# Turning two row groups of the first batch's spectrum by DMA transposes from a padded tile, and storing the last output rows in two column halves

## Chip, cores, metric

One core of one Trainium2 chip. The metric is the device time of one execution in microseconds (us), lower is better. Times are medians of several executions; all executions quoted here were in the fast state (one core has no die to compare with, and no run lay more than 1.5% above the fastest of its kernel).

## The reference

```python
X = np.fft.rfft(x, axis=1)                        # x: 8 x 3008 x 256, float32
y = np.fft.irfft(X * (filt_r + 1j*filt_i)[None], n=3008, axis=1)
x = y.reshape(24064, 256)
h = x @ w_in                                      # 256 x 2048
g = h * (1.0 / (1.0 + np.exp(-beta * h)))
out = g @ w_out                                   # 2048 x 256
```

## The kernel before

The transform along 3008 is done as a two-stage matrix DFT (64 x 47), in bfloat16. Each batch goes through first-stage products, a transpose, products with the filter between two stages (the "spectrum"), a turn to the other axis, and last products that give `y`. Then comes the two-layer network on `y`. Its unit is a step: two hidden matmuls into `hps`, a Silu on ScalarE, and, two steps later, four output matmuls into `acc`. A step takes TensorE about 0.87 us. (To evacuate is to copy a result out of PSUM, the memory that TensorE writes.) The transform of the next batches is cut into units which `place(first, last, units)` puts between the steps, so that TensorE never stops.

Only the first batch has nothing to hide behind. Its spectrum `z_t` is turned on TensorE, in four groups of 8 rows: group 0 at once, groups 1 to 3 between steps.

```python
    z_t = ypool.tile([P, NDC, J, KP], BF16, name="z_t", tag="y")     # KP = 96 of 128 columns
    ...
    def turn_z(g, i, on_act=False):                                  # half of a group
        if g not in zz0:
            zz0[g] = zzpool.tile([KP, JG, D], BF16, name="zz", tag="zz")
        pz = fpsum.tile([P, 4, D], BF16, name="pz", tag="f")
        for e in range(4):
            for dc in range(NDC):
                nc.tensor.transpose(
                    pz[:KP, e, dc * P : (dc + 1) * P], z_t[:, dc, JG * g + 4 * i + e, :], ident[:]
                )
        evac(zz0[g][:, 4 * i : 4 * i + 4, :], pz[:KP], on_act)       # PSUM to SBUF
    ...
    # one unit of a later batch's spectrum (s23): products, then two units later the inverse stage
            nc.vector.tensor_tensor(p_t[:], ps[:], frr[:, ks_, :], ALU.mult)   # frr: filter
            ...
            nc.gpsimd.tensor_tensor(v_t[:], p_t[:], q_t[:], ALU.add)
            ...
            evac(s["z"][:, kk : kk + 2, :], ps[:], True)             # z: pool of 2 buffers
            if kk + 2 == KG:
                nc.sync.dma_start(s["d2c"][:, g * KG : (g + 1) * KG, :], s["z"][:])
    ...
    place(1, 14, uz(1, True))          # turn + last products of group 1; True: ScalarE evacuates y
    place(15, 29, uz(2, True))
    units = uz(3, True)
    place(20, 24, units[:2], per=2)
    place(34, 58, units[2:])
    ...
        place(10, 10, uf(0, JG), per=9)                              # filter loads, on SyncE
        at = place(9, 14, units[J // 4 :], per=9)                    # second batch, first stage
        place(at + 1, at + 1, [lambda: a2_read(1)] + uf(JG, NK), per=9)   # 8 DMA transposes, loads
        ...
        place(36, 36, ux(2), per=9)                                  # third batch's x, on GpSimd
```

SyncE issues the filter loads, the DMA transposes, the stores of `z` and all output rows, and before the first filter load a small DMA, the "marker", that holds its queue until the second batch's `x` has landed. GpSimd issues the loads of `x`. A queue's "ring" is its row of transfers that are issued and not yet moved. "x load" below is the third batch's, unless said otherwise.

Of the kernel before, what the change touches and what calls it, by code (L numbers as in the profile page):

```python
# [39 lines left out]
def kernel(  # L40
# [396 lines left out]
    z_t = ypool.tile([P, NDC, J, KP], BF16, name="z_t", tag="y")  # L437
# [25 lines left out]
    def inverse3(i):  # L463
        k0 = 2 * i
        p_t, q_t = pq.pop(i)

        last = i == NK // 2 - 1
        for j0, j1 in ((0, JG), (JG, J)) if last else ((0, J),):
            nj = 4 * (j1 - j0)
            if j0:  # L470
                ps = fpsum.tile([P, 2, NDC, nj], F32, name="psz", tag="f")
            else:
                ps = opsum.tile([P, 2, NDC, nj], F32, name="psz", tag="acc")
            for src, tab in ((p_t, t3), (q_t, t3b)):
                for e in range(2):
                    for dc in range(NDC):
                        nc.tensor.matmul(  # L477
                            ps[:, e, dc, :],
                            lhsT=src[:, e, dc * P : (dc + 1) * P],
                            rhs=tab[:, k0 + e, 4 * j0 : 4 * j1],  # L480
                            start=src is p_t and dc == 0 and e == 0,
                            stop=src is q_t,
                            skip_group_check=True,
                        )
            for e in range(2) if last else (None,):
                if last:
                    dst = z_t[:, :, j0:j1, 4 * (k0 + e) : 4 * (k0 + e) + 4]
                    src = ps[:, e].rearrange("p c (j a) -> p c j a", a=4)
                else:
                    dst = z_t[:, :, :, 4 * k0 : 4 * k0 + 8].rearrange(  # L490
                        "p c j (e a) -> p e (c j) a", e=2
                    )
                    src = ps.rearrange("p e c (j a) -> p e (c j) a", a=4)
                evac(dst, src, not last or j0 > 0)
# [45 lines left out]
    zz0[0] = zz0[0][:KP, : JG * D].rearrange("p (j d) -> p j d", j=JG)  # L540


    def turn_z(g, i, on_act=False):
        if g not in zz0:
            zz0[g] = zzpool.tile([KP, JG, D], BF16, name="zz", tag="zz")
        pz = fpsum.tile([P, 4, D], BF16, name="pz", tag="f")
        for e in range(4):
            for dc in range(NDC):
                nc.tensor.transpose(  # L549
                    pz[:KP, e, dc * P : (dc + 1) * P], z_t[:, dc, JG * g + 4 * i + e, :], ident[:]  # L550
                )
        evac(zz0[g][:, 4 * i : 4 * i + 4, :], pz[:KP], on_act)

    def last4(zz, tab, jj, dc, dst, on_act, own=None, first=NP):
        ps = own or fpsum.tile([P, 4, P], F32, name="ps4", tag="f")
        for e in range(4):
            nc.tensor.matmul(  # L557
                ps[:, e, :NP],
                lhsT=zz[:, jj + e, dc * P : (dc + 1) * P],
                rhs=tab[:],  # L560
                start=True,
                stop=True,
            )
        rest = []
        for n0, n1 in ((0, NP),) if own is None or first == NP else ((0, first), (first, NP)):
            rest.append(
                lambda n0=n0, n1=n1: evac(
                    dst[:, n0:n1],
                    ps[:, :, n0:n1].rearrange("p j n -> p n j"),
                    on_act,  # L570
                    inv_scale,
                )
            )
        rest.pop(0)()
        return rest
# [9 lines left out]
    for i in range(4):  # L585
        if i % 2:
            pz = opsum.tile([P, 2, D], BF16, name="pz", tag="acc")
        else:
            pz = fpsum.tile([P, 2, D], BF16, name="pz", tag="f")
        for e in range(2):  # L590
            for dc in range(NDC):
                nc.tensor.transpose(
                    pz[:KP, e, dc * P : (dc + 1) * P], z_t[:, dc, 2 * i + e, :], ident[:]
                )
        evac(zz0[0][:, 2 * i : 2 * i + 2, :], pz[:KP], i % 2 == 1)
# [98 lines left out]
    def zz_read(b):  # L694
        s = st[b]
        s["zz"] = []
        for h in range(NJG):
            t = zzpool.tile([KP, JG, D], BF16, name="zz", tag="zz")
            nc.sync.dma_start(t[:], s["d2r"][:, h * JG : (h + 1) * JG, :])
# [46 lines left out]
    def uz(g, act=False):  # L746
        return [lambda i=i: turn_z(g, i) for i in range(2)] + [
            lambda i=i: last_z(g, i, act) for i in range(2 * NDC)
        ]
# [25 lines left out]
    place(1, 14, uz(1, True))  # L775
    place(15, 29, uz(2, True))
    units = uz(3, True)
    place(20, 24, units[:2], per=2)
    place(34, 58, units[2:])

    first_step = [(S * b // TB) * NFB for b in range(B + 1)]
    if B > 1:
        units = u1(1, True)
        place(3, 8, units[: J // 4], per=2)
        place(10, 10, uf(0, JG), per=9)
        at = place(9, 14, units[J // 4 :], per=9)
        place(at + 1, at + 1, [lambda: a2_read(1)] + uf(JG, NK), per=9)
# [51 lines left out]
    for s in range(len(steps) + LAG):  # L839
# [34 lines left out]
        if s >= LAG:  # L874
# [40 lines left out]
            if fb == NFB - 1:  # L915
                for h, a in enumerate(acc):
# [4 lines left out]
                    if last and h == nch - 1:  # L921
                        for half in range(2):
                            cols = slice(half * P, (half + 1) * P)
                            evac(ost[:, c : c + per, cols], a[:, :, cols], half == 1)
                    else:
                        evac(ost[:, c : c + per, :], a[:], on_act)
# [31 lines left out]
```

## Time and profile before

| | before |
|---|---|
| time, median of the first 3 runs | 776.72 us (776.48 to 778.47) |
| profiled span | 775.3 us |
| TensorE, ScalarE, VectorE busy | 99%, 77%, 49% |
| DMA engines' mean busy share, 64 to 80 us | 70% (below) |

### The profile page before, as it was taken

The page shows a single profiled execution, that of the slowest core. Times are in us where ns is not written, and L with a number is a line of the kernel's source. Part 1 is how long each engine was busy: PE and PEld are TensorE (multiplying, and loading weights), DVE is VectorE, ACT ScalarE, POOL GpSimd, SP SyncE. Part 2 cuts the span into 40 slices and gives each one's busy share as a digit, 9 for nine tenths or more (in the row PEclk, how much of TensorE's full clock was granted, in tenths as well). Part 3 has the DMA queues.
Part 4 walks back from the last instruction along what each step waited for, and adds up shares of the span by engine and source line. Part 5 has one row for each costly group of instructions (what it writes and reads, how often), then busy time and mean ns, then how long its engine had stood idle before and what let it go on. Part 6 is the DMA issues. An engine that isn't in the chain of part 4 may idle for free.

```text
span 775.3 us, 16219 instructions
## 1 busy us (share of the span) xinstructions
PE 767.5 (99%) x6444; PEld 554.2 (71%) x6444; DVE 379.3 (49%) x641; ACT 594.9 (77%) x926; POOL 142.8 (18%) x145
## 2 busy tenths in 40 slices
PE   8999999999999999999999999999999999999998
PEld 4877777777777777877768777787777776776665
DVE  7836846645446553474526735277353761401001
ACT  6888887886678867788677876778767787677776
POOL 7523401420013100231002410034000430000000
PEclk9999999999999999999999999999999999999999
DMA  7969755515911268022761237512451114100101
GB/s 170 240 164 191 169 164 106 136 55 155 177 43 68 89 145 161 30 85 85 160 134 47 78 116 146 106 64 80 130 110 55 49 69 129 56 28 28 55 28 55
DMA packets 103291, 80.48 MB, mean 104 GB/s; under 512 B 48466, under 2 KB 96996, under 8 KB 102258
## 3 DMA queue, kind: packets, MB, share of 16 engines
q1 hardware_dynamic: 100496, 63.73, 30.8%
q0 software_dynamic: 2720, 15.73, 10.5%
q8 instruction: 50, 0.82, 0.5%
q14 instruction: 25, 0.20, 0.1%
HBM read 46.15 MB, written 35.65 MB: 106 GB/s over the span
## 4 chain that ended last, share of the span: by engine, by line
PE 97%; ACT 1%; DMA 1%; POOL 0%; DVE 0%; issue 0%; POOLq 0%
PE acc L907 42%; PE hps L852 42%; PE ps L557 3%; PE ps L628 2%; PE ps L687 2%; PE ps L661 2%; DMA xg<-in_x_dram 1%; PE psz L477 1%; PE pz L549 0%; ACT a L109 0%; ACT a_t L109 0%; PE pb L403 0%; POOL xg L120 0%; PE ps L451 0%; PE ps2q L451 0%; PE pt L354 0%
## 5 line engine op out<-in xcount | busy, mean ns | idle before, releaser
L867 ACT ACTIVATE gT<-hps,beta_sb 128x512 bf16<-128x512 f32 x752 | 516.0, 688 | 166.8 <-PE hps L852 155.0
L907 PE MATMUL acc<-wout_sb,gT 128*128 128x256 bf16 x3008 | 451.6, 272 | 0.0
L852 PE MATMUL hps<-y,win_sb 128*128 128x512 bf16 (+8 forms) x1730 | 447.7, 351 | 0.0
L907 PEld LDWEIGHTS <-gT 128*128 128x128 bf16 x3008 | 279.6, 98 | 106.3 <-ACT gT L867 0.2
L852 PEld LDWEIGHTS <-win_sb 128*128 128x128 bf16 x1730 | 165.0, 98 | 24.4 <-issue 0.2
L677 POOL TENSOR_TENSOR v_t<-p_t,q_t 128x512 bf16<-128x512 f32 x84 | 106.7, 1270 | 383.9 <-DVE q_t L676 375.4
L111 DVE COPY ost<-acc 128x512 f32<-128x512 f32 (+2 forms) x89 | 56.6, 674 | 194.0 <-PE acc L907 188.4
L111 DVE CAST a<-ps 128x384 bf16<-128x384 f32 x96 | 53.5, 558 | 91.4 <-PE ps L628 91.2
L113 DVE TENSOR_SCALAR y<-ps 128x376 bf16<-128x376 f32 (+1 forms) x115 | 61.7, 544 | 59.5 <-PE ps L557 59.5
L672 DVE TENSOR_TENSOR p_t<-ps,frr 128x512 f32<-128x512 f32 x84 | 58.1, 692 | 33.5 <-PE ps L661 30.9
L676 DVE TENSOR_TENSOR q_t<-ps,fri 64x512 f32<-64x512 f32 x84 | 58.3, 694 | 1.2
L673 DVE SCALAR_TENSOR_TENSOR q_t<-ps,fri 64x512 f32<-64x512 f32 x84 | 57.4, 684 | 1.1
L557 PEld LDWEIGHTS <-zz 96*128 96x128 bf16 x512 | 35.3, 97 | 29.1 <-issue 0.3
L109 ACT ACTIVATE z<-ps 128x512 bf16<-128x512 f32 x84 | 49.6, 590 | 0.0
L628 PEld LDWEIGHTS <-xg 94*128 94x128 bf16 x448 | 30.7, 97 | 23.4 <-issue 0.4
L628 PE MATMUL ps<-t1b,xg 94*128 94x96 bf16 x448 | 36.7, 205 | 0.0
L557 PE MATMUL ps<-t,zz 96*128 96x94 bf16 x448 | 36.7, 204 | 0.0
L687 PE MATMUL ps<-v_t,t 128*128 128x256 bf16 x168 | 32.1, 273 | 0.0
L661 PE MATMUL ps<-a,t 128*128 128x256 bf16 x168 | 32.1, 273 | 0.0
L120 POOL DMA_DIRECT2D xg<-in_x_dram x22 | 12.1, 552 | 97.5 <-PE acc L907 93.9
L661 PEld LDWEIGHTS <-t 128*128 128x128 bf16 x168 | 15.7, 98 | 14.1
L687 PEld LDWEIGHTS <-t 128*128 128x128 bf16 x168 | 16.3, 98 | 6.4 <-DVE q_t L676 0.4
(118 smaller groups left out, 193.9 us busy)
## 6 DMA issues: line engine op xcount, KB each, us to landing
out_dram<-ost SPq DMA_DIRECT2D x80, 256.0 KB
d<-z SPq DMA_DIRECT2D x28, 384.0 KB
zz<-d SPq DMA_DIRECT2D x28, 384.0 KB
xg<-in_x_dram POOLq DMA_DIRECT2D x6, 1280.0 KB, 10.1
frr<-in_filt_r_dram SPq DMA_DIRECT2D x12, 256.0 KB
out_dram<-ost SPq DMA_DIRECT2D x20, 128.0 KB
frr<-in_moe_w_out_dram POOLq DMA_DIRECT2D x4, 512.0 KB, 12.8
xg<-in_x_dram POOLq DMA_DIRECT2D x6, 224.0 KB, 11.0
```

The source lines that it names most:

```text
L111: nc.vector.tensor_copy(dst, src)
L113: nc.vector.tensor_scalar_mul(dst, src, scale)
L557: nc.tensor.matmul(ps[:, e, :NP], lhsT=zz[:, jj + e, dc * P : (dc + 1) * P], rhs=tab[:], start=True, stop=True,)
L628: nc.tensor.matmul(ps[:, e, :KP], lhsT=s["x"][:, 4 * jq + e, dc * P : (dc + 1) * P], rhs=t1b[:], start=True, stop=True,)
L661: nc.tensor.matmul(ps[:, e, :], lhsT=t2[:, k0 + e, 3:5, :].rearrange("p c k -> p (c k)"), rhs=s["a2"][g][:, :, kk + e, :], start=True, sto ...
L672: nc.vector.tensor_tensor(p_t[:], ps[:], frr[:, ks_, :], ALU.mult)
L676: nc.vector.tensor_tensor(q_t[:M], ps[M:P], fri[M:P, ks_, :], ALU.mult)
L677: nc.gpsimd.tensor_tensor(v_t[:], p_t[:], q_t[:], ALU.add)
L687: nc.tensor.matmul(ps[:, e, :], lhsT=t3[:, k0 + e, :], rhs=v_t[:, e, :], start=True, stop=True)
L852: nc.tensor.matmul(hps[:, pos - t0 : pos - t0 + ln], lhsT=win_sb[:, dc, fb * P : (fb + 1) * P], rhs=ys[b][:, dc, n0 : n0 + ln], start=(dc ...
L867: nc.scalar.activation(gT[:, :tn], hps[:, :tn], ACT.Silu, scale=beta_sb[:, fb : fb + 1])
L907: nc.tensor.matmul(acc[tb // per][:, tb % per, :], lhsT=g_[:, tb * P : (tb + 1) * P], rhs=wout_sb[:, f_, :], start=(f_ == 0 and tb % per = ...
```

## The change

The intent: 48 transposes of groups 1 to 3 stand on TensorE, the bound. Groups 2 and 3 are taken off it. Here the DMA transposes are given whole blocks of 128x128, so `z_t` is padded from 96 to 128 columns with zeros, group 0 gets its own unpadded tile, and each evacuation of the spectrum is split in two. Filter loads move ahead of the second batch's transposes, apparently so that less stands in front of the group-3 transpose. At the end, the last 128 output rows leave in two halves over two queues. Core of the diff:

```diff
-    z_t = ypool.tile([P, NDC, J, KP], BF16, name="z_t", tag="y")
+    z_0 = a2pool.tile([P, NDC, JG, KP], BF16, name="z_0", tag="a2")
+    z_t = ypool.tile([P, NJG - 1, NDC, JG, P], BF16, name="z_t", tag="y")
+    gp.memset(z_t[:, :, :, :, KP:], 0.0)
     ...                                       # evacuation: z_0 and z_t apart (cut)
+    def read_z(g):
+        zz0[g] = zzpool.tile([P, NDC, JG, P], BF16, name="zz", tag="zz")
+        nc.sync.dma_start_transpose(
+            zz0[g].rearrange("p c j d -> p (c j) d"),
+            z_t[:, g - 1].rearrange("p c j r -> p (c j r)"),
+        )
     ...
-    place(1, 14, uz(1, True))
-    place(15, 29, uz(2, True))
-    units = uz(3, True)
-    place(20, 24, units[:2], per=2)
-    place(34, 58, units[2:])
+    place(1, 14, [lambda i=i: turn_z(1, i, True) for i in range(2)] + uz(1, True))
+    place(9, 9, [lambda: read_z(2)], per=9)
+    place(17, 29, uz(2, True))
+    place(38, 58, uz(3))                      # no True: VectorE evacuates group 3's y
     ...
-        place(10, 10, uf(0, JG), per=9)
+        place(10, 10, uf(0, 2 * JG), per=9)
         at = place(9, 14, units[J // 4 :], per=9)
-        place(at + 1, at + 1, [lambda: a2_read(1)] + uf(JG, NK), per=9)
+        place(at + 1, at + 1, [lambda: a2_read(1)] + uf(2 * JG, NK), per=9)
+        place(at + 1, at + 1, [lambda: read_z(3)], per=9)
     ...
-                        for half in range(2):
+                        for half, eng in ((0, nc.sync), (1, nc.scalar)):
                             cols = slice(half * P, (half + 1) * P)
-                            evac(ost[:, c : c + per, cols], a[:, :, cols], half == 1)
+                            ost = pqpool.tile([P, 2, D], F32, name="ost", tag="pq"[half] + "_t")
+                            evac(ost[:, :1, :P], a[:, :, cols], half == 1)
+                            eng.dma_start(out[TOK - P :, cols], ost[:, 0, :P])
```

More of the change, by code (lines that the diff above doesn't have):

```diff
@@ L468, in inverse3 @@
         for j0, j1 in ((0, JG), (JG, J)) if last else ((0, J),):
-            nj = 4 * (j1 - j0)
+            ng = (j1 - j0) // JG
             if j0:
-                ps = fpsum.tile([P, 2, NDC, nj], F32, name="psz", tag="f")
+                ps = fpsum.tile([P, 2, ng, NDC, 4 * JG], F32, name="psz", tag="f")
             else:
-                ps = opsum.tile([P, 2, NDC, nj], F32, name="psz", tag="acc")
+                ps = opsum.tile([P, 2, ng, NDC, 4 * JG], F32, name="psz", tag="acc")
             for src, tab in ((p_t, t3), (q_t, t3b)):
@@ L477, in inverse3 @@
                         nc.tensor.matmul(
-                            ps[:, e, dc, :],
+                            ps[:, e, :, dc, :],
                             lhsT=src[:, e, dc * P : (dc + 1) * P],
-                            rhs=tab[:, k0 + e, 4 * j0 : 4 * j1],
+                            rhs=tab[:, k0 + e, 4 * j0 : 4 * j1].rearrange(
+                                "p (g r) -> p g r", g=ng
+                            ),
                             start=src is p_t and dc == 0 and e == 0,
@@ L484, in inverse3 @@
                         )
-            for e in range(2) if last else (None,):
-                if last:
-                    dst = z_t[:, :, j0:j1, 4 * (k0 + e) : 4 * (k0 + e) + 4]
-                    src = ps[:, e].rearrange("p c (j a) -> p c j a", a=4)
-                else:
-                    dst = z_t[:, :, :, 4 * k0 : 4 * k0 + 8].rearrange(
-                        "p c j (e a) -> p e (c j) a", e=2
-                    )
-                    src = ps.rearrange("p e c (j a) -> p e (c j) a", a=4)
-                evac(dst, src, not last or j0 > 0)
+            for e0, ne in ((0, 1), (1, 1)) if last else ((0, 2),):
+                cols = slice(4 * (k0 + e0), 4 * (k0 + e0 + ne))
+                if j0 == 0:
+                    evac(
+                        z_0[:, :, :, cols].rearrange("p c j (e a) -> p e (c j) a", a=4),
+                        ps[:, e0 : e0 + ne, 0].rearrange("p e c (j a) -> p e (c j) a", a=4),
+                        not last,
+                    )
+                if j1 == J:
+                    evac(
+                        z_t[:, :, :, :, cols].rearrange("p g c j (e a) -> p e (g c j) a", a=4),
+                        ps[:, e0 : e0 + ne, (JG - j0) // JG :].rearrange(
+                            "p e g c (j a) -> p e (g c j) a", a=4
+                        ),
+                        True,
+                    )
     def table4():
@@ L539 @@
     zz0[0] = apool.tile([P, NK * P], BF16, name="zz", tag="a1")
-    zz0[0] = zz0[0][:KP, : JG * D].rearrange("p (j d) -> p j d", j=JG)
+    zz0[0] = zz0[0][:, : JG * D].rearrange("p (c j d) -> p c j d", c=NDC, j=JG)
     def turn_z(g, i, on_act=False):
         if g not in zz0:
-            zz0[g] = zzpool.tile([KP, JG, D], BF16, name="zz", tag="zz")
-        pz = fpsum.tile([P, 4, D], BF16, name="pz", tag="f")
-        for e in range(4):
-            for dc in range(NDC):
-                nc.tensor.transpose(
-                    pz[:KP, e, dc * P : (dc + 1) * P], z_t[:, dc, JG * g + 4 * i + e, :], ident[:]
-                )
-        evac(zz0[g][:, 4 * i : 4 * i + 4, :], pz[:KP], on_act)
+            zz0[g] = zzpool.tile([P, NDC, JG, P], BF16, name="zz", tag="zz")
+        pz = fpsum.tile([P, NDC, 4, P], BF16, name="pz", tag="f")
+        for dc in range(NDC):
+            for e in range(4):
+                nc.tensor.transpose(pz[:KP, dc, e, :], z_t[:, g - 1, dc, 4 * i + e, :KP], ident[:])
+        evac(zz0[g][:KP, :, 4 * i : 4 * i + 4, :], pz[:KP], on_act)
+    def read_z(g):
+        zz0[g] = zzpool.tile([P, NDC, JG, P], BF16, name="zz", tag="zz")
+        nc.sync.dma_start_transpose(
+            zz0[g].rearrange("p c j d -> p (c j) d"),
+            z_t[:, g - 1].rearrange("p c j r -> p (c j r)"),
+        )
     def last4(zz, tab, jj, dc, dst, on_act, own=None, first=NP):
@@ L558, in last4 @@
                 ps[:, e, :NP],
-                lhsT=zz[:, jj + e, dc * P : (dc + 1) * P],
+                lhsT=zz[:KP, dc, jj + e, :],
                 rhs=tab[:],
@@ L586 @@
         if i % 2:
-            pz = opsum.tile([P, 2, D], BF16, name="pz", tag="acc")
+            pz = opsum.tile([P, NDC, 2, P], BF16, name="pz", tag="acc")
         else:
-            pz = fpsum.tile([P, 2, D], BF16, name="pz", tag="f")
+            pz = fpsum.tile([P, NDC, 2, P], BF16, name="pz", tag="f")
         for e in range(2):
             for dc in range(NDC):
-                nc.tensor.transpose(
-                    pz[:KP, e, dc * P : (dc + 1) * P], z_t[:, dc, 2 * i + e, :], ident[:]
-                )
-        evac(zz0[0][:, 2 * i : 2 * i + 2, :], pz[:KP], i % 2 == 1)
+                nc.tensor.transpose(pz[:KP, dc, e, :], z_0[:, dc, 2 * i + e, :], ident[:])
+        evac(zz0[0][:KP, :, 2 * i : 2 * i + 2, :], pz[:KP], i % 2 == 1)
     pw[0] = hpsum.tile([P, TB], F32, name="pw", tag="hps")
@@ L697, in zz_read @@
         for h in range(NJG):
-            t = zzpool.tile([KP, JG, D], BF16, name="zz", tag="zz")
-            nc.sync.dma_start(t[:], s["d2r"][:, h * JG : (h + 1) * JG, :])
+            t = zzpool.tile([P, NDC, JG, P], BF16, name="zz", tag="zz")
+            t = t[:KP].rearrange("p c j d -> p (c j d)").rearrange("p (j c d) -> p c j d", c=NDC, j=JG)
+            nc.sync.dma_start(
+                t.rearrange("p c j d -> p j c d"),
+                s["d2r"][:, h * JG : (h + 1) * JG, :].rearrange("r j (c d) -> r j c d", c=NDC),
+            )
             s["zz"].append(t)
@@ L746, in uz @@
     def uz(g, act=False):
-        return [lambda i=i: turn_z(g, i) for i in range(2)] + [
-            lambda i=i: last_z(g, i, act) for i in range(2 * NDC)
-        ]
+        return [lambda i=i: last_z(g, i, act) for i in range(2 * NDC)]
     def uf(a, z):
@@ L921 @@
                     if last and h == nch - 1:
-                        for half in range(2):
+                        for half, eng in ((0, nc.sync), (1, nc.scalar)):
                             cols = slice(half * P, (half + 1) * P)
-                            evac(ost[:, c : c + per, cols], a[:, :, cols], half == 1)
-                    else:
-                        evac(ost[:, c : c + per, :], a[:], on_act)
+                            ost = pqpool.tile([P, 2, D], F32, name="ost", tag="pq"[half] + "_t")
+                            evac(ost[:, :1, :P], a[:, :, cols], half == 1)
+                            eng.dma_start(out[TOK - P :, cols], ost[:, 0, :P])
+                        continue
+                    evac(ost[:, c : c + per, :], a[:], on_act)
                     store(t0 + h * per * P, per * P, ost[:, c : c + per, :])
```

## The prediction

> **What bounds the kernel now.** I read the page's busy table first, then who waited for whom, then the order of time around the places that the diff touches. Busy table:
>
> ```profile
> PE 767.5 (99%) x6444; PEld 554.2 (71%) x6444; DVE 379.3 (49%) x641; ACT 594.9 (77%) x926; POOL 142.8 (18%) x145
> ```
>
> 99% is a modelled share, so I checked it with the waits whose waiter is TensorE. Those above 0.4 us are:
>
> ```profile
> PE pw L189 <- DVE wz L184: 1.2, 1, 1.2
> PE psa L305 <- DMA xg<-in_x_dram: 0.7, 2, 0.5
> PE pb L403 <- DVE a L111: 0.5, 1, 0.5
> PE ps2q L451 <- ACT t L109: 0.5, 1, 0.5
> PE bps L526 <- DVE qb_t L460: 0.5, 1, 0.5
> ```
>
> All of them lie before 36 us. From 36 us to the last matmul the matmul stream waits for nothing longer than a few tenths, and the chain that ended last is TensorE for 97% of the span. So after 36 us a TensorE instruction that is removed shortens the program by its pitch, and a wait put into that stream lengthens it by its length, because nothing afterwards has slack to win it back. Before 36 us the stages are shared: from 20 to 30 us TensorE, VectorE and ScalarE are busy 9.73, 9.43 and 9.56 of 10 us.
>
> TensorE's timeline around two of the transposes to be removed, and the first matmul of the second batch's spectrum:
>
> ```profile
> 53.83 0.59 PE L852 MATMUL hps<-y,win_sb 128*128 128x512 bf16 x2
> 54.26 0.61 PE L549 MATMUL pz<-ident,z_t 128*96 128x128 bf16 x8
> 54.71 0.60 PE L907 MATMUL acc<-wout_sb,gT 128*128 128x256 bf16 x4
> ...
> 59.67 0.61 PE L549 MATMUL pz<-ident,z_t 128*96 128x128 bf16 x8
> 60.12 0.60 PE L907 MATMUL acc<-wout_sb,gT 128*128 128x256 bf16 x4
> 60.55 0.59 PE L852 MATMUL hps<-y,win_sb 128*128 128x512 bf16 x2
> 60.98 0.38 PE L661 MATMUL ps<-a,t 128*128 128x256 bf16 x2
> ```
>
> A group of 8 transposes occupies 54.71 - 54.26 = 0.45 us of the stream, although its records overlap with the neighbours'.
>
> The other view that matters is the DMA queue of SyncE in time, because the change puts work into it:
>
> ```profile
> 46.60 0.23 SPq L521 DMA_DIRECT2D mark<-xg  x1
> 46.87 0.31 SPq L133 DMA_DIRECT2D frr<-in_filt_r_dram  x1
> ...
> 48.18 0.42 SPq L136 DMA_DIRECT2D frr<-in_filt_r_dram  x1
> 52.97 12.04 SPq L648 DMA_TRANSPOSE a<-a  x8
> ```
>
> The queue stands still until 46.60 (its marker waits 24.3 us for the x load), issues four filter loads of 256 KB, waits for the second batch's first-stage result, and then issues 8 transposes of 128x768. The median issue is 1.29 us for 6 blocks of 128x128, so 0.215 us a block.
>
> **What the Trainium skill says.** "DMA: Bandwidth & Descriptors", section "Queues, rings and completion order", states that each issuing queue owns one ring per DMA engine and that descriptors are consumed there in ring order. This trace agrees: from 65.18 us SyncE issues eight filter loads (2 MB), the DMA share stays near full until about 75.5 us, and only then do the output rows behind them move. VectorE pays, since its copy into a reused output buffer starts only at 77.53:
>
> ```profile
> 77.53 0.69 DVE L111 COPY ost<-acc 128x512 f32<-128x512 f32 x1 [2.37 <-ACT z L109]
> ```
>
> (The named releaser has nothing to do with that buffer; the stores of its last user have.) "VectorE: DVE Perf Modes", section "The three transpose paths", gives 390 ns for a TensorE transpose of 128x128 and 1309 ns for one by DMA. In this stream I measure 0.45 / 8 = 56 ns and 0.215 us, so both are far cheaper here, and the trace's numbers are used. "PSUM — Partial Sum Buffer", section "PSUM bank collisions raise a hardware error", says that two engines must not touch one bank and quadrant together, reads included. The trace's tail agrees: ScalarE copies its half of the last accumulator only when VectorE has ended its half.
>
> **The change part by part.**
>
> Removed: the turning of groups 2 and 3, which is 4 units of 8 transposes on TensorE (at 54.26, 56.45, 59.67 and 64.20 us), 4 x 0.45 = 1.8 us off the binding stream. Their four VectorE copies (0.69 us each) go too, but VectorE is 49% busy and off the path: worth 0.
>
> Moved to ScalarE: the two copies of group 1's turn, 96x1024. From 128x768 in 0.82 us and 96x512 in 0.59 us I get about 1.03 us each (an estimate). ScalarE has 1.38 us of idle just before 41.92 us; TensorE's fourth following hidden block then finds its buffer free with 0.3 us to spare. I count +0.1.
>
> Split: each of the 11 full evacuations of the spectrum becomes two on ScalarE. From 128x192 (0.33 us) and 128x512 (0.59 us), 128 and 384 columns take 0.28 and 0.49. Successive copies overlap by about 0.08, so an iteration costs ScalarE 0.1 us more, 1.1 in all. In the first nine iterations ScalarE would have about 9 x 0.59 + 9 x 0.72 = 11.8 us to do, VectorE 9 x 1.2 + 3 x 0.46 = 12.2, so VectorE stays the pace. The first group's turn can start some 0.2 us sooner after the last matmul because it now waits for the small copy alone. Net +0.1.
>
> The memset of the padding (1536 columns, GpSimd) falls into its idle 1.57 us before 22.39 us: 0.
>
> Added on SyncE's queue: two transposes of 16 blocks, 16 x 0.215 = 3.4 us of issue each, and four of the filter loads move ahead of the second batch's transposes (eight there now instead of four). The new order from 46.9 us is: group 2's transpose to 50.3; eight loads issued by 54.1; then the second batch's transposes. Group 2 lands near 51.5 us and is wanted at about 57: hidden. But the eight loads are 2 MB, which took about 9.5 us when they stood together before; starting at 51 they end near 60.5. The first two spectrum transposes then need 1.4 us and are complete near 62. Before, they had landed by 57, for a use at 60.98. With three turns gone ahead of it, TensorE now gets to that use at 60.98 - 1.35 = 59.6. Worked plainly the stream waits 2.3 us. I count 1.7, since the queue model may be pessimistic: the load rate varies, and the padding transposes may issue faster than by blocks.
>
> Group 3's transpose comes after all that: queue free near 70, four remaining loads, data near 77 to 78; its first use is step 38, which in the old trace ran at about 77.5. I count 0.1. Output rows behind it land later by perhaps 2 us, which VectorE's three-iteration lag should absorb: 0.
>
> Tail: VectorE's half ends at 771.95, ScalarE's at 772.26, and one 128 KB store follows. Two stores of 64 KB on two queues let the first half go early, but the second copy still waits for the same bank. I count -0.2, mainly for the smaller last transfer.
>
> Sum: -1.8 + 0.1 + 0.1 + 1.7 + 0.1 - 0.2 = 0.0 on 776.72. Since the kernel is tuned and its author could see a wait of this size, I lean a little to the good side: 776.4.
>
> **The rivals.** First, all transposes are hidden: the spectrum arrives in time, and the kernel gains its 1.8 plus the tail, 774.5 to 775. For it: the DMA engines stand idle from 52.6 to 54.2 us, and later loads move out of the way of the output rows. Against it: ring order, as shown at 77.53. Second, the wait comes in full and is followed by another for group 3 and by VectorE's late output copy, which holds back the products for the next inverse stage: 2.3 + 1 to 2 us of waits against 2 of gain, 778 to 779. For it: VectorE already lagged 2.7 us behind its matmul at 78.25. Against it: that lag cost TensorE nothing before. Third, ScalarE's extra copies become the bound from 20 to 30 us: +1 us, so 777.5. For it: 9.56 of 10 busy. Against it: VectorE's count above. In each case the second batch onwards is untouched: its reads keep their bytes and layout, and only the first batch's turn is taken from TensorE.
>
> **Range and chances.** The first rival gives the low end, the second the high: 774.3 to 778.6. No term here comes near 2% (15.5 us), which would need a stall an order larger than any in this trace; faster by 2% is impossible from 1.8 us of removed work. Chances 0.005, 0.985, 0.01.
>
> **What would show it.** The turn line should have 16 TensorE transposes left of 48. The first spectrum matmul of the second batch (two 128x256 at 60.98 before) should start at about 61 to 62 with a wait on a DMA; if it starts at 59.6 without one, the first rival is right and I am about 1.7 us too slow. SyncE's queue should show the new transposes at about 3.4 us of issue. From 20 to 36 us the stage should end within 0.3 us of before: the first hidden-layer matmul stood at 37.00. The last two copies should still be one after the other. I am wrong altogether if a wait appears in later batches, or if the filter loads run much faster beside the transposes than alone.

## More of the kernel before

The prediction shows TensorE's waits and the timelines around the turns. Two more readings of the kernel before are needed for what follows. The first is the DMA row of the stretch from 64 to 80 us, in 40 slices; a digit is the mean busy share of the 16 DMA engines in tenths:

```profile
DMA  9059494689995969996979997979999999820027
```

TensorE is not alone near its limit here. From the ninth slice (67.2 us) to the 35th (78 us) the digits average 8.3: the DMA engines are close to full as well. The second is when SyncE issues the first store of `z`, and when GpSimd issues the x load (columns: start in us, duration in us, queue, line, operation, tiles, count):

```profile
79.58 0.54 SPq L692 DMA_DIRECT2D d<-z  x1
...
81.73 1.10 POOL L120 DMA_DIRECT2D xg<-in_x_dram  x2
```

The store is 2.15 us ahead of a load of 1504 KB (1280 and 224).

## The result

| | before | after |
|---|---|---|
| time, median of 6 runs | 776.41 us (775.91 to 778.47) | 782.73 us (781.77 to 784.62) |
| profiled span | 775.3 us | 781.1 us |

The changed kernel is correct and slower: ratio 1.008 (95% interval 1.0063 to 1.0096), 4.1 us above the top of the predicted range. A ratio here is the mean time of one kernel's runs over the mean of the other's in the same rounds, so it is not quite the ratio of the medians quoted.

Busy table of the kernel after, then the two longest waits of TensorE in it (columns of the waits: waiter, waited for, us in total, times, longest):

```profile
PE 767.5 (98%) x6412; PEld 553.2 (71%) x6412; DVE 377.1 (48%) x639; ACT 595.4 (76%) x935; POOL 144.0 (18%) x146
```

```profile
PE ps L675 <- DMA a<-a: 3.6, 1, 3.6
PE hps L868 <- ACT gT L883: 2.9, 1, 2.9
```

TensorE lost the intended 32 instructions (6444 to 6412), and two waits stand in the stream where none was.

**First wait.** TensorE's timeline of the kernel after; a bracket gives the idle time before and its releaser:

```profile
57.11 0.82 PE L923 MATMUL acc<-wout_sb,gT 128*128 128x256 bf16 x6
57.86 0.59 PE L868 MATMUL hps<-y,win_sb 128*128 128x512 bf16 x2
62.02 0.61 PE L675 MATMUL ps<-a,t 128*128 128x256 bf16 x2 [3.57 <-DMA a<-a]
62.42 1.06 PE L923 MATMUL acc<-wout_sb,gT 128*128 128x256 bf16 x4
...
65.17 0.59 PE L868 MATMUL hps<-y,win_sb 128*128 128x512 bf16 x2
```

Two hidden matmuls take 0.43 us of the stream, so TensorE is ready for the second batch's first spectrum product at 57.86 + 0.43 = 58.29, and starts it at 62.02: 3.7 us. SyncE's queue in the kernel after shows why:

```profile
46.44 1.75 SPq L565 DMA_TRANSPOSE zz<-z_t  x1
...
52.49 15.65 SPq L662 DMA_TRANSPOSE a<-a  x8
70.23 5.03 SPq L565 DMA_TRANSPOSE zz<-z_t  x1
75.36 8.25 SPq L842 DMA_DIRECT2D out_dram<-ost  x10
83.70 5.94 SPq L706 DMA_DIRECT2D d<-z  x2
```

Eight filter loads stand between the group-2 transpose and the eight transposes that feed the spectrum, and those now take 15.65 us to issue instead of 12.04. Everything behind comes later too: `z` is stored from 83.70 instead of 79.58. (It is SyncE's queue that holds the store: the last copy into its tile ended at 79.88.)

The wait has an echo. Stretches of the kernel after (columns: length, then busy us and instruction count of TensorE, weight loads, VectorE, ScalarE, GpSimd; granted TensorE clock; DMA share summed over its queues' packets; GB/s):

```profile
58.00:62.00 4.00, 0.45 (x2) 0.00 (x0) 0.00 (x0) 1.07 (x2) 0.00 (x0) 0.95 1.25 204
62.00:65.00 3.00, 2.98 (x15) 1.90 (x16) 2.07 (x3) 0.57 (x1) 0.16 (x1) 0.50 1.11 117
65.00:68.00 3.00, 3.00 (x24) 2.08 (x23) 1.10 (x2) 2.05 (x5) 1.11 (x1) 0.99 0.68 152
```

After the idle stretch the granted clock is 0.50 for three us. The Trainium skill, "TensorE: Matmul & The Clock Gate", section "Part 1: The HAM clock gate (the "warmup" mystery)", says that the array falls to half its clock after an idle window of about 3.4 us and needs about as long of work to come back. This trace agrees. From 62.02 to 65.17, 3.15 us, TensorE does 2 spectrum products, 4 last products, 8 output and 2 hidden matmuls, worth 1.70 us at the pitches of full clock: another 1.45 us lost. This part differs from run to run: the mean granted clock of the six runs lies between 0.993 (784.62 us) and 1.000 (781.77 us), and is 0.998 in the profiled one.

**Second wait.** It ends at 96.77, and is at bottom a wait of ScalarE for a `z` buffer (first TensorE's, then ScalarE's, then GpSimd's timeline of the kernel after):

```profile
93.22 0.60 PE L923 MATMUL acc<-wout_sb,gT 128*128 128x256 bf16 x4
96.77 0.59 PE L868 MATMUL hps<-y,win_sb 128*128 128x512 bf16 x2 [2.94 <-ACT gT L883]
```

```profile
95.54 0.60 ACT L109 ACTIVATE z<-ps 128x512 bf16<-128x512 f32 x1 [3.54 <-DMA d<-z]
```

```profile
82.55 1.10 POOL L120 DMA_DIRECT2D xg<-in_x_dram  x2
```

ScalarE cannot copy into the third `z` tile until the store of the first has landed (two buffers). Its Silu is behind that copy, so the hidden layer stops: 96.77 - (93.22 + 0.44) = 3.1 us. The store is only 384 KB. But it is now issued at 83.70, after the x load (82.55), where it had been issued before it. What the two DMA queues moved in two windows of 1 us of the kernel after, 88 to 89 and 94 to 95 us (q0: GpSimd's queue, with the x load; q1: SyncE's; columns: packets, MB, share of the engines' time):

```profile
q0 software_dynamic: 15, 0.25, 119.7%
q1 hardware_dynamic: 16, 0.02, 5.9%
...
q1 hardware_dynamic: 153, 0.41, 103.1%
```

Beside the x load SyncE's queue moves 0.02 MB in a microsecond; once the load is through it moves 0.41. The Trainium skill, "DMA: Bandwidth & Descriptors", section "Queues, rings and completion order", says that an engine takes turns between queues packet by packet. This window agrees: 15 packets against 16, but one side's packets have 16 KB and the other's have under 2 KB. Over the whole load, 84 to 92 us, the trace counts 108 packets against 84, and none of SyncE's from 85 to 88, so the turns are not even throughout. In the kernel before, the store went first, at up to 0.28 MB per us:

```profile
q1 hardware_dynamic: 193, 0.28, 74.4%
```

(q1 of the kernel before, 80 to 81 us; q0 moves nothing there.)

**What went as predicted.** The groups' rows of the kernel after for 37 to 43 us, then for 20 to 37 us (busy us, mean ns, idle before):

```profile
L109 ACT ACTIVATE zz<-pz 96x1024 bf16<-96x1024 bf16 x2 | 2.1, 1028 | 0.0
```

```profile
L109 ACT ACTIVATE z_t<-psz 128x384 bf16<-128x384 f32 x11 | 5.5, 503 | 0.0
L109 ACT ACTIVATE z<-psz 128x128 bf16<-128x128 f32 x11 | 3.1, 285 | 1.1 <-PE psz L480 1.1
```

The last copies of the kernel after are still one behind the other, and the two stores leave together:

```profile
777.67 0.29 DVE L111 COPY ost<-acc 128x128 f32<-128x128 f32 x1 [0.40 <-PE acc L923]
777.99 0.28 ACT L109 ACTIVATE ost<-acc 128x128 f32<-128x128 f32 x1 [1.21 <-DVE ost L111]
778.23 0.41 SPq L942 DMA_DIRECT2D out_dram<-ost  x1
778.30 0.37 ACTq L942 DMA_DIRECT2D out_dram<-ost  x1
```

**The account**, from TensorE's timelines of the two profiled runs:

| term | us |
|---|---|
| first hidden matmul, 37.00 to 36.41 (first x load landed earlier in this run; from the first spectrum matmul to it 20.30 before, 20.32 after) | -0.6 |
| four half-group turns gone | -1.8 |
| wait for the spectrum's transposes | +3.7 |
| half clock after it | +1.45 |
| wait for the `z` store, through ScalarE | +3.1 |
| tail: start of the last output matmuls to the end, 6.15 to 6.0 | -0.1 |
| sum (spans: 781.1 - 775.3) | +5.8 |

### The profile page after: what moved, and what is told of

The parts are those of the page before. It is cut to its first block, busy times and chain, and to the rows that moved or that the text cites. A ratio compares the mean times of both kernels' runs of the same rounds, so it can differ in the third digit from the quotient of the medians.

```text
span 781.1 us, 16165 instructions
## 1 busy us (share of the span) xinstructions
PE 767.5 (98%) x6412; PEld 553.2 (71%) x6412; DVE 377.1 (48%) x639; ACT 595.4 (76%) x935; POOL 144.0 (18%) x146
## 4 chain that ended last, share of the span: by engine, by line
PE 95%; DMA 2%; ACT 2%; DVE 0%; issue 0%; DVEq 0%; ACTq 0%
PE acc L923 42%; PE hps L868 41%; PE ps L573 3%; PE ps L642 2%; PE ps L675 2%; PE ps L701 2%; DMA a<-a 1%; DMA d<-z 1%; PE pw L189 1%; PE psz L480 1%; ACT a_t L109 0%; ACT a L109 0%; PE pb L403 0%; ACT r L284 0%; ACT t L280 0%
## 5 line engine op out<-in xcount | busy, mean ns | idle before, releaser
L113 DVE TENSOR_SCALAR y<-ps 128x376 bf16<-128x376 f32 (+1 forms) x119 | 63.9, 545 | 61.6 <-PE ps L573 61.6
```

Of the source, the lines that this page charges most:

```text
L113: nc.vector.tensor_scalar_mul(dst, src, scale)
```

## The experiments

Theory A: the moved filter loads make the first wait, and what is late behind them makes the second. Rival: the DMA transposes themselves, or another part of the change (layout, evacuation on VectorE), carry the loss. Each edit is given against the kernel named. All twelve kernels gave correct results. "Before" is the median of the kernel before, run beside it.

### Loads back alone; loads moved alone

Edit of the kernel after:

```diff
-        place(10, 10, uf(0, 2 * JG), per=9)
+        place(10, 10, uf(0, JG), per=9)
-        place(at + 1, at + 1, [lambda: a2_read(1)] + uf(2 * JG, NK), per=9)
+        place(at + 1, at + 1, [lambda: a2_read(1)] + uf(JG, NK), per=9)
```

> The changed kernel with the filter loads split as before (four ahead of the second batch's spectrum transposes, eight behind). Theory A (ring order: what stands ahead of those transposes decides when the spectrum lands): only 1 MB stands ahead, so the spectrum's first group lands near 57 us, the wait of 3.6 us at the first spectrum matmul and the slow clock after it go, worth 5.2 us. The output rows and the first two stores of the z tiles then stand behind 2 MB and group 3's transpose, so the second wait (ScalarE's z copy for the store of z, 3.5 us) stays or grows: 776 to 779 in all. Rival B (the padded transposes themselves slow the DMA engines or the spectrum transposes): the first wait stays above 2 us and the time stays near 782.

Measured: 782.32 us (before 775.88), ratio 1.0082 (1.0067 to 1.0097). The first wait is gone, and the second too. In their place stand two others, in TensorE's timeline of this run:

```profile
80.08 0.50 PE L573 MATMUL ps<-t4b,zz 96*128 96x94 bf16 x4 [3.43 <-DMA zz<-z_t]
83.45 0.61 PE L701 MATMUL ps<-v_t,t 128*128 128x256 bf16 x2 [2.44 <-DVE q_t L690]
```

With eight loads ahead of it, group 3's transpose takes 7.51 us to issue and is wanted before it lands. The expected time was missed by 3 us or more, and the second wait, which was to stay or grow, went: the wait moved, the sum stayed.

Edit of the kernel before: the same two lines the other way (`uf(0, 2 * JG)` early, `uf(2 * JG, NK)` late), nothing else.

> The kernel before with only the filter loads moved: eight ahead of the spectrum transposes, four behind; all turns still on TensorE. Theory A: the loads start at 46.9 us, are through by about 57, the spectrum's first group lands near 58.5, before its use at 61: no wait, time within 1 us of before, possibly 0 to 0.3 us better. If the loads alone are enough to hold up the spectrum (rival), a wait of 1 to 3 us appears at the first spectrum matmul and the time is 778 to 780.

Measured: 776.01 (before 775.88), ratio 1.0004 (0.9989 to 1.0019), no wait at the spectrum. As expected: moved loads without the transposes cost nothing. So the loads are needed for the first wait, but are not enough: in the kernel after, group 2's transpose stands ahead of them too, and TensorE asks for the spectrum at 58.29, where it asks at 61.34 here.

### Group 3 turned by TensorE

Edit of the kernel after:

```diff
+    place(20, 24, [lambda i=i: turn_z(3, i) for i in range(2)], per=2)
-        place(at + 1, at + 1, [lambda: read_z(3)], per=9)
```

> The changed kernel with group 3 turned by TensorE again, so one DMA transpose (group 2) is left. Theory: the first wait stays almost as it is (3.6 us less about 0.45, since one TensorE turn is back ahead of the use, with the slow clock after it); the second wait, which I put down to group 3's transpose pushing the output rows and the store of z behind the third batch's x load, goes. Time 783 - 3 + 0.9 = 780 to 781. Rival: the second wait comes from the first one's delay alone; then it stays near 3 us and the time is 783 to 784.

Measured: 778.79 (four runs: 778.34, 782.71, 776.13, 779.23), ratio 1.0044 (1.0006 to 1.0082). In the profiled run the first wait is 0.71 us: the second batch's x load ended early and the marker (44.47) let SyncE go 1.5 us sooner than in the kernel after (46.02). When that load lands varies from run to run, and so does the wait. The spectrum landed at 60.26. A run further down with both transposes in (the kernel after, `y` on ScalarE) has the same landing, 60.27, and a wait of 2.18 us: the other 1.5 us are TensorE's later arrival with group 3's turns back in front. What I had not expected is that the wait on `z` stayed (2.74 us on ScalarE), with group 3's transpose gone. SyncE and GpSimd in this run:

```profile
78.74 7.10 SPq L706 DMA_DIRECT2D d<-z  x2
...
78.61 1.10 POOL L120 DMA_DIRECT2D xg<-in_x_dram  x2
```

The store is issued earlier than in the kernel before; but the x load is 0.13 us ahead of it. Theory A's second half fell. Its successor: not how late the store is, but whether it is issued ahead of the x load.

### The x load moved

Edit of the kernel after: `place(36, 36, ux(2), per=9)` becomes `place(44, 44, ux(2), per=9)`. (A third buffer for `z`, the more direct test, did not fit the on-chip memory: the build stops for lack of space. It was not run.)

> The changed kernel with the third batch's x load placed 8 hidden blocks later (step 44 instead of 36). Theory: the second wait is the x load's large packets, which started at 84 us just as the first store of z was issued at 83.7; with the load later, the store of z lands near 85 us and the wait of 2.9 us at the hidden matmul goes: about 779.8, unless the later x load makes the third batch's first stage wait, which the trace would show as a wait on xg. Rival: the store of z is late by itself because its queue is; then the wait stays about 3 us.

Measured: 787.33 (before 775.88), ratio 1.0148 (1.0131 to 1.0165). The wait on `z` is gone, as the new theory says (store at 83.23, x load at 92.73). The wait for the spectrum is still 3.96 us. But x is now late for its own use, which costs more than it saved:

```profile
104.50 0.80 PE L642 MATMUL ps<-t1b,xg 94*128 94x96 bf16 x8 [7.65 <-DMA xg<-in_x_dram]
```

### One transpose, loads where they were

Edit: the kernel of the group-3 experiment, with the loads back (the two lines of the first experiment). One DMA transpose, group 2's, is left.

> The changed kernel with group 3 turned by TensorE and the filter loads split as before: one DMA transpose is left, ahead of four loads, in the 6 us in which SyncE's queue stood idle before. Theory (all of the loss is the order in SyncE's ring): no wait at the first spectrum matmul, none at zz, none at z; the two TensorE turns of group 2 are saved, 0.9 us, and up to 0.2 us at the tail: 1.0 us better than before, 0.9987 to 0.9992. Rival (splitting the evacuations or the copies on ScalarE cost time too): the same or slower than before, 1.000 or above.

Measured: 778.09 (before 776.09), ratio 1.0022 (1.0009 to 1.0035). Missed: I expected a gain. Neither old wait is there, but a product that passes through VectorE is late by 2 us:

```profile
80.25 0.49 PE L701 MATMUL ps<-v_t,t 128*128 128x256 bf16 x2 [2.03 <-DVE q_t L690]
```

VectorE's output copy waits for an output buffer until 77.38, no later than in the kernel before (77.53), so the buffer alone is not the cause. What differs is that in this kernel VectorE evacuates group 3's `y` in the same stretch, which ScalarE did before. The profiled run is the slowest of the five (779.89): after this wait the granted clock was 0.50 from 81 to 83 us. The mean clock of the five lies between 0.997 and 1.000, so not every run has this echo.

### Two ways of moving the loads out of the ring's way

Edit of the kernel after: the last 8 loads go on GpSimd's queue, at steps 18 to 21 and 24 to 27, and the first 4 stay (core; the two old `place` calls lose these loads).

```diff
+        place(18, 21, uf(JG, 2 * JG, gp), per=9)
+        place(24, 27, uf(2 * JG, NK, gp), per=9)
```

> Both DMA transposes kept; four filter loads on SyncE ahead of the spectrum transposes as before, the other eight issued by GpSimd (its own ring) at steps 18 to 21 and 24 to 27, so that only spectrum transposes and group 3's transpose stand ahead of the output rows on SyncE's ring. Theory: no wait for zz or z, the output rows land by about 73 us, 1.8 us saved on TensorE: 1.8 to 2.2 us better than before (0.9972 to 0.9977). Rival (total DMA traffic, not ring order, is what delays the spectrum): the spectrum or group 3 still comes late, the wait at the first spectrum matmul or at zz stays above 1.5 us, and the time is no better than before.

Measured: 781.34 (777.61 to 783.04; before 776.09), ratio 1.0058 (1.0036 to 1.008). Theory missed, and the rival's mark, one of the old waits above 1.5 us, did not appear either. The waits for the spectrum's transposes and for group 3 shrink to 0.8 and 0.7 us with the loads out of SyncE's ring, but VectorE now stands still for an output buffer, and TensorE then for VectorE's product (3.6 us):

```profile
79.46 0.69 DVE L111 COPY ost<-acc 128x512 f32<-128x512 f32 x1 [5.51 <-DMA out_dram<-ost]
```

The Trainium skill, "DMA: Bandwidth & Descriptors", section "Issuing engines are not separate DMA queues", says that transfers run on the same 16 DMA engines whoever starts them. This run is in line with that, without showing it: the loads were out of the output rows' ring, and the output buffer still came free later than in the kernel before (79.46 against 77.53). Nor did the edit keep the order that it was meant to: GpSimd does not wait for TensorE's steps and issued two of its loads at 45.40 and 45.98, just ahead of group 2's transpose, which now took 3.90 us to issue instead of 1.75.

Edit of the kernel after: four loads each at step 10, with the transposes at step 15, and at step 20.

```diff
-        place(10, 10, uf(0, 2 * JG), per=9)
+        place(10, 10, uf(0, JG), per=9)
-        place(at + 1, at + 1, [lambda: a2_read(1)] + uf(2 * JG, NK), per=9)
+        place(at + 1, at + 1, [lambda: a2_read(1)] + uf(JG, 2 * JG), per=9)
+        place(20, 20, uf(2 * JG, NK), per=9)
```

> Both DMA transposes kept and all loads on SyncE, but in thirds: four ahead of the spectrum transposes, four between them and group 3's transpose, four behind the first output rows. Theory: the spectrum lands near 56.5 us (no wait), group 3 near 73 (use near 75.5: no wait), and the first store of z comes behind four loads and ten output stores near 82, at the edge of the third batch's x load: either 1.8 us better than before, or a wait of 2 to 3 us for z and then 1 us slower.

Measured: 782.08 (before 776.09), ratio 1.0076 (1.0064 to 1.0088). No wait for the spectrum, none for group 3, but 4.7 us of TensorE behind ScalarE's wait on `z` (5.27 us). The store was issued at 81.32, the x load at 78.83: the order rule again. Of the two outcomes expected it is the second, but 5.9 us slower and not 1.

### The other parts of the change alone

Edit of the kernel after: both DMA transposes out, their turns back on TensorE at the old steps, loads back, group 3's `y` on ScalarE. What remains is padding, layout, split evacuations, group 1's copies on ScalarE, and the tail.

```diff
-    place(9, 9, [lambda: read_z(2)], per=9)
-    place(17, 29, uz(2, True))
-    place(38, 58, uz(3))
+    place(15, 29, [lambda i=i: turn_z(2, i) for i in range(2)] + uz(2, True))
+    place(20, 24, [lambda i=i: turn_z(3, i) for i in range(2)], per=2)
+    place(34, 58, uz(3, True))
-        place(at + 1, at + 1, [lambda: read_z(3)], per=9)
```

> The changed kernel without either DMA transpose and with the loads as before: groups 2 and 3 are turned by TensorE where they were; left are the padded tile with its memset, the split evacuations, group 1's copies on ScalarE and the two column halves at the tail. Theory: within 0.3 us of before (0.9996 to 1.0003), from first spectrum matmul to first hidden matmul 20.3 us as before. Rival: these parts cost 1 us or more (1.0013 or above).

Measured: 776.42 (before 776.09), ratio 1.0002 (0.999 to 1.0014), none of the waits. As expected: all parts but the transposes and the loads cost and gain nothing that five rounds can see.

### Who evacuates group 3's y

Edit of the one-transpose kernel: `place(38, 58, uz(3))` becomes `place(34, 58, uz(3, True))`.

> The one-transpose version (group 2 by DMA, group 3 by TensorE, loads as before), with group 3's last evacuations given back to ScalarE and to their old steps (34 to 58), as in the kernel before. Theory: the 2.0 us wait of the inverse matmul for VectorE's product came because group 3's evacuation, moved to VectorE by the change, held one of three PSUM buffers while VectorE stood still for its output buffer until about 77.4 us; with it on ScalarE that wait goes, nothing else waits, and 0.9 us of TensorE turns is saved: 0.9985 to 0.9995. Rival: being 0.9 us earlier is itself too early, since the output rows land at the same moment as before; then VectorE's lag grows to more than three iterations and a wait of 0.5 to 2 us stays at the inverse matmul: 1.000 or above.

Measured: 776.40 (before 776.20), ratio 0.9995 (0.9979 to 1.0012). VectorE's product wait is gone. Group 2's two turns, 2 x 0.45 = 0.9 us, are still saved on TensorE, and are given back in one place, so the theory's "nothing else waits" missed, though its rival's wait for VectorE did not come either:

```profile
93.09 0.50 PE L642 MATMUL ps<-t1b,xg 94*128 94x96 bf16 x8 [1.08 <-DMA xg<-in_x_dram]
```

TensorE got there sooner; the x load did not.

Edit of the kernel after: the same evacuation on ScalarE, `place(38, 58, uz(3, True))`.

> The changed kernel, group 3's last evacuations on ScalarE instead of VectorE, nothing else. In the changed kernel the waits are for the spectrum (3.6 us) and for z (2.9 us), not for VectorE's product, so I expect no gain: 781.5 to 783.5, with both waits as they were. If the time falls by 2 us or more, VectorE's load was a cause in the change too.

Measured: 782.00 (before 776.20), ratio 1.0062 (1.0038 to 1.0087). Both waits are there (2.18 and 3.60 us), and one of 0.82 us for ScalarE's copy of `y`. As expected, in the change itself this choice of engine is not the cause.

### x two steps earlier

Edit of the previous section's first kernel: `place(36, 36, ux(2), per=9)` becomes `place(34, 34, ux(2), per=9)`, to remove its last wait. And the same edit of the kernel before, as the control.

> The version with one DMA transpose and group 3's evacuations on ScalarE, with the third batch's x load placed two hidden blocks earlier (step 34), so that GpSimd issues it ahead of the product that waits for VectorE's late output copy: issue near 75 to 76 us instead of 81. Theory (the 0.9 us saved on TensorE came back as the 1.1 us wait for this load): the load lands by about 88 to 90, the wait on it goes, and the time is 0.9 to 1.1 us under before (0.9985 to 0.9990). Rival (the DMA engines are full from 53 to 93 us, so an earlier load only pushes something else): a wait for z, for the output buffer or for VectorE's product takes its place and the time is no better than before.

Measured: 776.55 (before 776.42), ratio 1.0000 (0.9988 to 1.0013). The wait for x is gone, and 0.8 us of TensorE behind ScalarE's wait for `z` is back, since x (75.25) is now issued ahead of the store (79.15). (The profile puts ScalarE's 1.40 us before that copy, at 89.24, down to a hidden matmul, which the copy does not read; SyncE's queue was moving the store until then, 0.40 MB from 87 to 88 us.) The rival expectation was right.

> The kernel before with only the x load moved to step 34. It had no wait on this load, so there is nothing to gain: the same as before within 0.5 us if the earlier load disturbs nothing; if the DMA engines are full there, a wait for z or for the output buffer appears and it is 1 to 3 us slower.

Measured: 777.66 (before 776.42), ratio 1.0019 (1.0005 to 1.0032). The kernel before, which had no such wait, gets it from this one placement (x load at 75.36, store at 78.62), in ScalarE's timeline:

```profile
89.13 0.60 ACT L109 ACTIVATE z<-ps 128x512 bf16<-128x512 f32 x1 [1.04 <-DMA d<-z]
```

This is the cleanest evidence for the second wait. One placement in a kernel without the change makes it. The profiled run is the fastest of its five (776.49) and TensorE loses only 0.44 us in it, so the 1.2 us between the medians is not traced in full. All fourteen profiles sort by the order: ScalarE waits for the `z` store where the x load is issued first, and only there (x at step 34 with one transpose as read above). Order and not distance sorts them: with the load 0.53 us behind the store (loads moved alone; 79.90, 79.37) or 0.23 behind (loads back alone; 84.77, 84.54) there is no wait, with it 0.13 ahead there are 2.74 us. Nine of them:

| kernel | `z` store issued | x load issued | ScalarE's wait for `z` |
|---|---|---|---|
| before | 79.58 | 81.73 | none |
| one transpose, loads back | 79.42 | 81.57 | none |
| the same, `y` on ScalarE | 78.91 | 81.07 | none |
| after, x load at step 44 | 83.23 | 92.73 | none |
| after | 83.70 | 82.55 | 3.54 us |
| group 3 turned by TensorE | 78.74 | 78.61 | 2.74 us |
| after, loads in thirds | 81.32 | 78.83 | 5.27 us |
| after, `y` on ScalarE | 81.88 | 80.75 | 4.20 us |
| before, x load at step 34 | 78.62 | 75.36 | 1.04 us |

## Why the prediction was wrong

It said 776.4 with 778.6 as the top; it is 782.7. Step by step:

- **Removed work, -1.8: right.** The account closes with it in full; it is lost again elsewhere.
- **Evacuations split (+0.1), copies on ScalarE (+0.1), memset (0), tail (-0.2): not contradicted.** Their sum of 0.0 fits the layout experiment, 1.0002, which can see about 0.9 us. The stage with the split took 20.32 us (20.30 before), and the tail won 0.15; the others were not measured singly. The estimate of 1.03 us for the copy of 96x1024 measured 1.028.
- **"The first two spectrum transposes ... are complete near 62": right (62.02), but in part by luck.** It gave group 2's transpose 3.4 us of issue, which took 1.75 (group 3's, held up, took 5.03), so the loads began at 48.26 and not at 50.3. Their packets gave way to the transposes' small ones near 59 and not 60.5, and the first two transposes then took about 3 us and not 1.4. The two errors cancel. **"TensorE now gets to that use at 60.98 - 1.35 = 59.6": wrong.** It got there at 58.29. Of the 1.3 us, 0.6 is the earlier start of this run, and the other 0.7 is about one step (0.87): with group 3's turns gone, `place` found room in step 20, and the first spectrum unit moved up into it from step 21. Removing work from a schedule that fills free slots pulls other work forward, to before its data is there.
- **"Worked plainly the stream waits 2.3 us. I count 1.7": the wrong direction to round.** The wait was 3.7, and the half clock after it, which no term covered, makes it 5.2. This is 3.5 of the 6.3 us by which the prediction missed.
- **"Output rows behind it land later by perhaps 2 us, which VectorE's three-iteration lag should absorb: 0": failed.** I followed the queue to the output rows and no further. Behind them in the same ring stood the store of `z`, 4.1 us later than before, and this put it behind the x load of another queue: +3.1. The second rival came nearest, with its "another" wait, but named the wrong one and stopped at 779.
- **"In each case the second batch onwards is untouched": wrong** in time, true in bytes. Both waits are in the second batch's spectrum. The sentence on what would make it wrong altogether, "a wait [...] in later batches", came true.
- **Not seen at all:** the change moves group 3's evacuations of `y` from ScalarE to VectorE. In the change itself it is hidden; in the version with one transpose it costs the product wait (1.0022 against 0.9995 without it). Which buffer hands that delay on is not settled.

Why no variant gained: shown is that between 58 and 105 us several transfers each arrive just in time. Take 0.9 or 1.8 us off TensorE, and it meets one of them (`a` transposes, group 3, `z` store, x load). In every experiment that took a wait away and kept a DMA transpose, another wait came up at a transfer or buffer further on (group 3 turned by TensorE apart, where the second wait simply stayed). That the DMA engines' capacity in this stretch is the common limit behind all of them is my reading of their full slices and of the two load experiments; no run reduced the bytes without also changing an order. Part of each loss is half clock again: in the profiles of six of the variants it follows a TensorE wait, so a variant's time is more than the sum of its waits.

None of the versions beats the kernel before: the best, 0.9995, has an interval that contains 1.

## What to carry to other kernels

Before moving work from the busiest engine to a DMA queue, read how full the DMA engines are in that stretch, and follow everything behind the new transfer in its ring, to the last buffer that someone waits for, including its order against big loads on other queues. In a schedule that fills free slots, work out anew when each transfer's consumer will ask for it. And a wait of a few us can cost more than its length, because TensorE may resume at half clock: here it did after waits of 2.03 and of 3.43 us and more, and did not after waits of 2.14, 2.18 and 2.94 (the second wait, 3.1 by the pitches).

## What the Trainium skill lacked or had wrong

- "VectorE: DVE Perf Modes", the three transpose paths: the table gives the time of one transpose, 1309 ns by DMA and 390 ns on TensorE for 128x128, and no rate for many in a row, which is what a plan like this needs. Here 16 blocks on an empty ring were issued in 1.75 us (0.11 us a block; issue, not landing), and TensorE's ran at 0.45 / 8 = 56 ns.
- "DMA: Bandwidth & Descriptors" does not say in the sections read that a transpose's issue is held up by what stands ahead in its ring. The same transpose took 1.75 us with nothing ahead, 5.03 us behind four late filter loads and the spectrum's transposes, and 7.51 us behind eight loads. It is not the ring alone: with nothing ahead in its ring but two loads of GpSimd's queue moving, it took 3.90 us.
- The same page states arbitration by packets, but not what follows for a small-packet store beside a big-packet load: 16 packets against 15, and 0.02 MB against 0.25 MB in the same microsecond (in other microseconds of the load the store moved no packet); 384 KB issued at 83.70 released its buffer only at about 95.5.
- "TensorE: Matmul & The Clock Gate": the account of the idle window fits (3.7 us idle, then clock 0.50 for three us). The second wait, 3.1 us, left the clock at 1.00; the page's free-running window of 3.4 us allows that. What it does not account for is the kernel with one transpose and the loads back: its profile shows a wait of 2.03 us, with TensorE busy on both sides, and then a clock of 0.50 from 81 to 83 us. Its "Part 4: PE-mode transpose" says that transposes do not engage the full clock; here eight between matmuls kept the pitch of 56 ns, which is too short a stretch to test it.
